# Transposing the activations of two of nine units by DMA in 16-bit halves instead of on TensorE

## The chip, the cores and the metric

The kernel runs on one core of one Trainium2 chip. The metric is the time of one execution on the device, in microseconds (us). Before the change it is 636.36 us, the median of 3 runs (635.49 to 636.7).

## What is computed

The reference is an attention followed by a dense layer pair and a soft mixture of experts:

```python
attn_out = _attn_ref(q, k, v, tau)            # 4 batches, 8 heads, 576 tokens, head size 64
x = attn_out.transpose(0, 2, 1, 3).reshape(2304, 512)
g = np.maximum(x @ w_in, 0.0) ** 2            # 2304 x 2048
x = g @ w_out                                 # 2304 x 512
logits = x @ phi                              # 32 slots
d = softmax(logits over the 2304 tokens)
slot_input = d.T @ x                          # 32 x 512, four slots for each of 8 experts
slot_out[e] = np.maximum(slot_input[e] @ w1[e], 0.0) @ w2[e]     # 512 -> 1024 -> 512
out = softmax(logits over the slots) @ slot_out                  # 2304 x 512
```

All inputs and outputs are 32-bit floats.

## The kernel before

**Units.** The 2304 tokens go through the dense layers in nine units of 256 tokens: two for each of the four batches, (0, 0) to (3, 1), and a last one, "rem", with the 64 tokens left over of each batch. So the seventh and eighth unit are the two of the last batch; the ninth is "rem". In each unit TensorE (PE) multiplies the split weights w_in with the unit's x (L1176, operations f_a and f_b, eight pairs; one pair gives 256 of the 2048 columns of g, transposed: columns of g on the partitions, the unit's 256 tokens along the free axis). ScalarE (ACT) applies relu (L1185) and square (L1193) into a tile `gt` of 128 x 512. There are nine gt buffers, and a unit has eight such tiles, so the next unit can begin only one pair before buffers of this one have to come free.

**The step after each unit.** `post` (L971) adds the rest of a unit's work, which is carried out while the next unit's f_a and f_b run. f_pl and f_pm (L982) multiply g with w_out @ phi for the logits; f_p12 and f_p1k (L989, L995) sum and turn them; f_alpha (L1005) takes the exponential; f_p3 (L273, L1041) turns the result, and DVE copies it to `dk` and `ar` (L1045, L1048). In place of x, the kernel accumulates d.T @ g (32 x 2048, in `sg`) and multiplies by w_out only at the end (L1344). For that g is needed with tokens on the partitions. f_turn transposes it on PE (L273, called from L1075): for each half t of the 256 tokens and each j of 0 to 3, four transposes of 128 x 128 into one PSUM tile, 32 transposes per unit. f_gk evacuates each of the eight PSUM tiles to a tile `gk` (L1083 on ACT, L1085 on VectorE (DVE) in part of the ninth unit); there are four gk buffers. f_acc (L1098) multiplies with dk, f_merge (L1107) adds into sg. The turns of t = 1 release the gt buffers.

**Order.** A planner at build time (class `Plan`) holds all operations of attention and of the units with their engine, a cost, dependencies, keys and buffers to acquire and release. It steps through time and starts on each free engine the ready operation with the lowest key; the order that comes out is the order of each engine's instructions, which the chip then executes with semaphores. For a DMA it keeps a `bus`, occupied for the given `dma` time; SP issues only while the bus is booked no further ahead than DQ = 2.212 us, and a DMA given with a negative time (a transpose) also holds SP's place:

```python
if o.dma:
    self.bus = max(self.bus, self.now + DMA_LEAD) + o.dma      # DMA_LEAD = 1.13
    o.end = max(self.bus, o.end + DMA_LEAD) + DMA_TAIL         # DMA_TAIL = 0.95
    if o.turn:
        self.free[o.eng] = max(self.now + o.cost, self.bus - DMA_TAIL)
```

**DMA transposes today.** In attention, the probabilities of the batches after the first, split into two 16-bit parts of 128 x 2304 (`hl`), are already transposed by DMA on SP's queue (dturn, L779), 48 times.

**Loads of the experts' part.** Eight tiles `raw64` (128 x 4 KB per partition) serve w_in, w_out, then q and k, and at last eight loads of 512 KB of w_out rows (w_pre, planned behind the stores of w_out; L1243). When attention is planned to its end, nine loads of 1 MB and one of 512 KB of expert rows (`ew8`, `ew6`) are issued at once into the memory that attention used; loads into buffers of x (`wx`) and of w_in (`w8`) are planned as these come free. The part after the units (`tail`) is written in program order: L1344 multiplies sg by the w_out rows, L1366 is the experts' first layer, L1421 the second, L1440 the output; further loads wait there for buffers that these steps release.

Of the kernel before, what the change touches and what calls it, by code (L numbers as in the profile page):

```python
# [147 lines left out]
def tile_kernel(  # L148
# [31 lines left out]
    RB = 8  # L180
# [21 lines left out]
    PORT = {('w_id', 'POOL'), ('low', 'POOL'), ('w_times', 'POOL'), ('w_rest', 'POOL'), ('spread', 'POOL'), ('c_low', 'POOL'), ('keep', 'DVE'), ('xhi', 'DVE'), ('xlo', 'DVE'), ('c_low', 'DVE'), ('c_shift', 'DVE'), ('w_lo', 'DVE'), ('v_lo', 'DVE'), ('q_lo', 'DVE')}  # L202
    FKEY = 1e5
    GKL = (1, 3)
    GKD = ()
# [84 lines left out]
    def row512(dt=F32, tag="gk", bufs=GB):  # L290
        return rows.tile([128, 512], dt, tag=tag, name=tag, bufs=bufs)

    def gt_tile():
        return fs.tile([128, 2 * NU], F32, tag="gt", name="gt", bufs=MC // 2 + 1)
# [10 lines left out]
    def conv_ops():  # L305
# [168 lines left out]
        for n in range(RB):  # L474
            add("w_pre", "SP", 0.5, lambda: state["wr"](), stores, 1000.0 + n, ["raw64"], dma=1.46)

# [484 lines left out]
    def ffn_ops(units):  # L961
# [8 lines left out]

        def post(u, d, first, last):  # L971
            w, po = {}, {}
# [92 lines left out]
            if not last:  # L1065
                codes(bk)
            lastsg, turns = fo.get("sg"), []
            for t in range(T):
                gks, ro = [], []
                for j in range(NG):  # L1070
                    def turn(t=t, j=j):
                        po[t, j] = mm_tile()
                        for i in range(MC // NG):
                            m = (MC // NG) * j + i
                            transpose(po[t, j][:, i * 128:(i + 1) * 128], d["gt"][m][:, t * 128:(t + 1) * 128])  # L1075

                    own = last and t == T - 1
                    tag = "cv" if own else "gk"

                    def evac(t=t, j=j, own=own, tag=tag):  # L1080
                        gk = w["gk", t, j] = row512(F32, "cv", CB) if own else row512()
                        if j not in gkd:
                            nc.scalar.activation(gk, po[t, j], AF.Copy)  # L1083
                        else:
                            nc.vector.tensor_copy(gk, po[t, j])  # L1085

                    rel = [("gt", d["rl"][2 * j + x]) for x in range(2)] if t == T - 1 else []
                    takes = ["mm", tag]
                    tt = add("f_turn", "PE", 0.47, turn, d["sq"], pk(), takes, rel)
                    gks.append((tag, tt))  # L1090
                    dv = j in gkd
                    ro.append(add("f_gk", "DVE" if dv else "ACT", 0.6 if dv else 0.49, evac, [tt], HI + 2, rel=[("mm", tt)]))
# [34 lines left out]
        for n, u in enumerate(units):  # L1127
# [33 lines left out]
            for m2 in range(MC // 2):  # L1161
# [21 lines left out]
                def relu(m2=m2, d=d, o=o, down=down):  # L1183
                    g = o["g"] = gt_tile()
                    nc.scalar.activation(g, o["h"], AF.Relu, scale=down)  # L1185
                    d["gt"][2 * m2], d["gt"][2 * m2 + 1] = g[:, 0:NU], g[:, NU:2 * NU]
# [20 lines left out]
            plan.release(ms[-1], [("xh", hs[0]), ("xl", ls[0])])  # L1207
            pending = lambda u=u, d=d, n=n: post(u, d, n == 0, n == len(units) - 1)
        pending()
# [252 lines left out]
    with tc.manual_schedule():  # L1462
        with ExitStack() as ph:
# [9 lines left out]
            W, take, ew8, ew6, wr, wx, w8, wg = weights()  # L1473
            state["wr"] = wr
            conv_ops()
            attn_ops()
# [5 lines left out]
        state["ew"] = ctx.enter_context(tc.tile_pool(name="ew", bufs=9, side="right"))  # L1482
        for f in [ew8] * 9 + [ew6]:
            f()
        for n in range(XPB + 1):
# [40 lines left out]
```

## Time and profile before

| | before |
|---|---|
| median of 3 runs | 636.36 us (635.49 to 636.7) |
| profiled execution, its own time | 636.38 us |
| its span in the trace | 634.6 us |
| PE busy | 580.7 us (92%) |
| DVE, ACT, POOL busy | 435.1, 438.9, 283.7 us |
| attention's last step | ends at 480.6 us |
| f_pl of seventh, eighth, ninth unit | at 495.7, 526.7, 557.7 us |
| L1344, first step with w_out rows | at 570.1 us |
| last load of expert rows lands | at 615.0 us |

Times in the trace are counted from the start of the span; the rows sit in engines' lanes named PE, PEld (weight loads of PE), DVE, ACT, POOL and SP (which issues the DMAs; SPq is its queue). A name such as `gk<-mm` is the tile written and the tile read. "Share" of the DMA is the mean over the core's 16 DMA engines.

### The profile page before, as it was taken

What the parts mean: (1) busy time and instruction counts of PE and PEld (TensorE: products, weight loads), DVE (VectorE), ACT (ScalarE), POOL (GpSimd) and SP (SyncE); (2) the same over time, 40 slices, a digit from 0 to 9 for tenths busy, and PEclk for the clock granted to TensorE, in tenths of its full rate; (3) what the DMA queues carried; (4) which work ended last, traced back from release to release, by engine and by line L of the source; (5) the groups of instructions that cost most, each with busy time, mean ns of one, the idle gap of its engine ahead of it and who ended that gap; (6) DMA issues with size and microseconds to landing.
All of it is one profiled execution on the core that took longest, in us unless ns stands there. A gap on an engine that the chain in (4) does not pass through costs nothing.

```text
span 634.6 us, 14115 instructions
## 1 busy us (share of the span) xinstructions
PE 580.7 (92%) x5218; PEld 405.8 (64%) x5218; DVE 435.1 (69%) x1230; ACT 438.9 (69%) x846; POOL 283.7 (45%) x464
## 2 busy tenths in 40 slices
PE   3897979989999999999999989999999999989972
PEld 1454546667777677667767667867868787854322
DVE  5798998999988987886888977897640302042133
ACT  3797757688888888988988878887864545431012
POOL 1446672267577766676756767765530000010000
PEclk9999888999999999999999999999999999999987
DMA  8975516667787867595856747787656911568957
GB/s 279 354 224 170 189 67 207 212 180 174 210 145 160 184 134 140 97 195 100 185 106 118 175 91 151 125 181 165 144 76 254 400 77 34 173 223 325 419 222 297
DMA packets 150324, 116.78 MB, mean 184 GB/s; under 512 B 119920, under 2 KB 128880, under 8 KB 148080
## 3 DMA queue, kind: packets, MB, share of 16 engines
q1 hardware_dynamic: 150256, 115.88, 67.3%
q8 instruction: 41, 0.67, 0.4%
q14 instruction: 27, 0.22, 0.1%
HBM read 73.72 MB, written 8.91 MB: 130 GB/s over the span
## 4 chain that ended last, share of the span: by engine, by line
PE 61%; DVE 15%; DMA 7%; ACT 6%; POOL 5%; issue 3%; SPq 1%; DVEq 0%; ACTq 0%; POOLq 0%
PE mm L1176 27%; PE mm L273 8%; PE s L707 6%; DMA w<-in_moe_w_dram 5%; PE po L876 5%; DVE u L733 4%; DVE e L749 4%; PE mm L1098 2%; POOL hl L772 2%; PE po L868 2%; PE mm L982 2%; ACT e L745 2%; PE s L694 2%; PE po L881 1%; DMA qt<-in_q_dram 1%
## 5 line engine op out<-in xcount | busy, mean ns | idle before, releaser
L1176 PEld LDWEIGHTS <-w 128*128 128x128 f16 x1728 | 166.5, 98 | 26.8 <-issue 7.9
L772 POOL TENSOR_TENSOR hl<-e,hl 128x288 f16<-128x288 f32 x192 | 147.2, 791 | 39.0 <-issue 28.5
L1176 PE MATMUL mm<-xh,w 128*128 128x256 f16 x1152 | 149.6, 273 | 0.3 <-ACT gk L1083 0.2
L749 DVE SCALAR_TENSOR_TENSOR e<-u,sm,e 128x576 f32<-128x576 f32 x144 | 120.1, 850 | 18.9 <-ACT e L745 14.7
L745 ACT ACTIVATE e<-u,sm 128x576 f32<-128x576 f32 x144 | 109.1, 770 | 20.3 <-DVE u L733 15.1
L739 POOL TENSOR_SCALAR sm<-sm,tau_p 128x1 f32<-128x1 f32 x144 | 72.9, 512 | 70.4 <-DVE u L733 64.3
L1176 PE MATMUL mm<-xl,w 128*128 128x256 f16 x576 | 86.4, 273 | 0.0
L1185 ACT ACTIVATE gt<-mm,scl 128x512 f32<-128x512 f32 x72 | 49.2, 683 | 53.4 <-PE mm L1176 52.8
L733 DVE TENSOR_SCALAR_CACHE_REDUCE u<-s,raw 128x576 f32<-128x576 f32 x90 | 71.1, 811 | 14.2 <-PE s L707 13.2
L768 ACT ACTIVATE hl<-e 128x576 f16<-128x576 f32 x96 | 64.0, 676 | 1.7 <-DVE e L749 1.5
L836 POOL TENSOR_SCALAR sm<-sm 128x4 f32<-128x4 f32 (+1 forms) x48 | 20.4, 426 | 61.1 <-DVE e L749 51.5
L1193 ACT ACTIVATE gt<-gt 128x512 f32<-128x512 f32 x72 | 45.0, 625 | 1.1
L733 DVE TENSOR_SCALAR_CACHE_REDUCE u<-s,nscale 128x576 f32<-128x576 f32 x54 | 42.6, 807 | 3.7 <-PE s L694 3.2
L1318 POOL MEMSET cv<- 128x512 f32 x4 | 1.9, 526 | 96.5 <-PE mm L1098 96.5
L816 ACT ACTIVATE pt<-mm 128x512 f32<-128x512 f32 x48 | 28.5, 601 | 19.8 <-PE mm L273 19.3
L1083 ACT ACTIVATE gk<-mm 128x512 f32<-128x512 f32 x66 | 35.3, 593 | 7.2 <-PE mm L273 7.0
L707 PEld LDWEIGHTS <-qt 128*128 128x128 f16 (+3 forms) x400 | 21.9, 99 | 28.5 <-issue 18.0
L273 PE MATMUL mm<-ident_r,e 128*128 128x128 f32 (+1 forms) x224 | 37.4, 301 | 2.8 <-DVE e L749 2.2
L273 PE MATMUL mm<-ident_r,gt 128*128 128x128 f32 x288 | 38.0, 278 | 0.2 <-ACT gk L1083 0.2
L273 PEld LDWEIGHTS mm<-ident_r,e 128*128 128x128 f32 (+1 forms) x224 | 28.1, 154 | 15.6 <-DVE e L749 5.4
L273 PEld LDWEIGHTS mm<-ident_r,gt 128*128 128x128 f32 x288 | 31.7, 143 | 8.0 <-issue 6.0
L876 PE MATMUL po<-pt,vh 128*64 128x256 f16 x576 | 36.0, 275 | 0.0
(196 smaller groups left out, 974.5 us busy)
## 6 DMA issues: line engine op xcount, KB each, us to landing
w<-in_moe_w_dram SPq DMA_DIRECT2D x17, 1024.0 KB, 14.0
w<-in_moe_w_dram SPq DMA_DIRECT2D x26, 512.0 KB, 8.7
raw<-in_moe_w_in_dram SPq DMA_DIRECT2D x16, 511.8 KB, 6.7
raw<-in_moe_w_out_dram SPq DMA_DIRECT2D x16, 511.8 KB, 4.1
raw<-in_v_dram SPq DMA_DIRECT2D x20, 256.0 KB, 3.4
w_out<-cv SPq DMA_DIRECT2D x16, 256.0 KB, 2.6
w<-w_out SPq DMA_DIRECT2D x8, 512.0 KB, 4.2
kt<-in_k_dram SPq DMA_DIRECT2D x10, 320.0 KB, 3.6
```

The lines of the kernel that those rows point to most:

```text
L273: nc.tensor.transpose(out_, in_, ident[:n, :n])
L707: nc.tensor.matmul(o0, d["qh"][r, a, q0], kk, start=full, stop=not full)
L733: nc.vector.tensor_scalar(u, o["s"][:, s0:s0 + S], d.get("nscale", nscale), None, ALU.mult, ALU.min, accum_out=gd["sm"][:, c:c + 1])
L739: nc.gpsimd.tensor_scalar(sm[:, 4 + c:5 + c], sm[:, c:c + 1], tau_p, None, ALU.add)
L745: nc.scalar.activation(e, o["u", a], AF.Exp, scale=-1.0, bias=gd["sm"][:, c:c + 1])
L749: nc.vector.scalar_tensor_tensor(e, o["u", a], sm[:, 4 + c:5 + c], e, ALU.is_le, ALU.mult, accum_out=sm[:, 8 + c:9 + c])
L768: nc.scalar.activation(o["hl"][:, a * S:(a + 1) * S], o["e"][:, a * S:(a + 1) * S], AF.Copy)
L772: nc.gpsimd.tensor_tensor(o["hl"][:, 2 * S:][:, i], o["e"][:, i], o["hl"][:, i], ALU.subtract)
L876: nc.tensor.matmul(po[64 * a:64 * a + 64, :n_], d["vh"][:, y, c0:c0 + D], gd["pt"][:, :, c + 5 * a + m, :], start=i == 0 and m == 0, stop= ...
L1176: nc.tensor.matmul(o["h"][:, i * NU:(i + 1) * NU], a, c, start=n_ == 0, stop=n_ == len(terms) - 1)
L1185: nc.scalar.activation(g, o["h"], AF.Relu, scale=down)
L1193: nc.scalar.activation(g, g, AF.Square)
```

## The change

For the seventh and eighth unit (`DTU = (6, 7)`, counted from 0) g is not transposed on PE. For each j, two f_part on ACT copy the two gt tiles of a pair, taken as 16-bit words, into one raw64 tile, upper and lower halves of each word apart; f_move transposes that tile of 128 x 2048 words by one DMA on SP into a second raw64 tile; f_join on DVE puts the halves together again into gk, in two copies for each t and j. gt buffers are released by f_part and f_pm. The w_out loads get a later key and stand behind these in the line for raw64 (which rows they load is fixed ahead, in `wo`), and the ew loads are planned as operations, with a place on the bus, instead of being issued at once.

```diff
+    DTU = (6, 7)
+    DEA = (0, 1)
...
+    def row512x2():
+        return rows.tile([128, 4 * CW], U16, tag="raw64", name="raw64", bufs=RB)
...
-            add("w_pre", "SP", 0.5, lambda: state["wr"](), stores, 1000.0 + n, ["raw64"], dma=1.46)
+            add("w_pre", "SP", 0.5, lambda n=n: state["wr"](state["wo"][n]), stores, 2 * FKEY + n, ["raw64"], dma=1.46)
...
+            halves = {}
+            for j in range(NG) if by_halves else ():
+                o = {}
+
+                def part(x, j=j, o=o):
+                    t = row512x2()
+                    if not x:
+                        o["h"] = t.rearrange("p (h x n) -> p h x n", h=2, x=2)
+                    else:
+                        o["t"] = t.rearrange("p (b f) -> p b f", f=128)
+                    g = d["pair"][2 * j + x].bitcast(U16).rearrange("p (n h) -> p h n", h=2)
+                    if x in DEA:
+                        nc.scalar.activation(o["h"][:, :, x], g, AF.Copy)
+                    else:
+                        nc.vector.tensor_copy(o["h"][:, :, x], g)
+
+                def move(j=j, o=o):
+                    nc.sync.dma_start_transpose(out=o["t"], in_=o["h"].rearrange("p h x n -> p (h x n)"))
+
+                hs = []
+                for x in range(2):
+                    eng = "ACT" if x in DEA else "DVE"
+                    hs.append(add("f_part", eng, 1.05 if x in DEA else 1.13, lambda x=x, f=part: f(x), [d["sq"][2 * j + x]] + hs[:1],
+                                  pk(), ["raw64"]))
+                    plan.release(hs[x], [("gt", d["rl"][2 * j + x])])
+                    plan.release(a, [("gt", d["rl"][2 * j + x])])
+                halves[j] = o, add("f_move", "SP", 1.0, move, hs, HI, [], [("raw64", hs[0])], dma=-3.5), hs[1]
             for t in range(T):
                 gks, ro = [], []
                 for j in range(NG):
...
+                    if by_halves:
+                        def join(t=t, j=j):
+                            gk = w["gk", t, j] = row512()
+                            y = gk.bitcast(U16).rearrange("p (m f h) -> p h m f", m=4, h=2)
+                            z = halves[j][0]["t"].rearrange("p (h m t) f -> p t h m f", h=2, t=T)[:, t]
+                            for h in range(2):
+                                nc.vector.tensor_copy(y[:, h], z[:, h])
+
+                        rel = [("raw64", halves[j][2])] if t == T - 1 else []
+                        r = add("f_join", "DVE", 1.2, join, [halves[j][1]], pk(), ["gk"], rel)
+                        gks.append(("gk", r))
+                        ro.append(r)
+                        continue
...
-            pending = lambda u=u, d=d, n=n: post(u, d, n == 0, n == len(units) - 1)
+            pending = lambda u=u, d=d, n=n: post(u, d, n == 0, n == len(units) - 1, n in DTU)
...
+            state["wo"] = [take(1024) for _ in range(RB)]
...
-        for f in [ew8] * 9 + [ew6]:
-            f()
+        for n, f in enumerate([ew8] * 9 + [ew6]):
+            add("w_load", "SP", 0.5, f, [], n - 100, dma=2.6 if f is ew8 else 1.3)
```

## Rows read from the trace of the kernel before

**Rows 1.** The page: busy time of PE, and its row of 40 slices.

```profile
PE 580.7 (92%) x5218; PEld 405.8 (64%) x5218; DVE 435.1 (69%) x1230; ACT 438.9 (69%) x846; POOL 283.7 (45%) x464
...
PE   3897979989999999999999989999999999989972
```

**Rows 2.** Stretches from f_pl to f_pl, and the tail: length, engines busy, PEclk, DMA share, GB/s.

```profile
495.70:526.68 30.98, 30.57 (x284) 24.49 (x283) 6.30 (x21) 15.92 (x29) 0.00 (x0) 1.00 0.49 191
526.68:557.65 30.97, 30.56 (x284) 24.48 (x283) 5.24 (x17) 15.91 (x29) 0.00 (x0) 1.00 0.36 120
...
583.00:615.00 32.00, 28.12 (x218) 9.16 (x210) 8.34 (x27) 2.96 (x6) 0.00 (x0) 0.95 0.91 371
```

**Rows 3.** The chain that ended last: start, length, what (seventh unit's post; the tail).

```profile
497.84 1.02 PE mm L273 x8
...
499.97 0.91 PE mm L273 x8
500.88 2.62 PE mm L1176 x24
...
505.41 1.90 PE mm L273 x16
...
570.12 3.57 PE mm L1344 x32
...
583.26 0.22 SPq L1243
...
583.57 16.09 DMA w<-in_moe_w_dram
```

**Rows 4.** The page's group of g's transposes; PE's timeline at the seventh unit's first f_acc.

```profile
L273 PE MATMUL mm<-ident_r,gt 128*128 128x128 f32 x288 | 38.0, 278 | 0.2 <-ACT gk L1083 0.2
...
504.34 1.06 PE L1098 MATMUL mm<-gk,dk 128*32 128x512 f32 x8 [0.41 <-DVE ar L1048]
```

**Rows 5.** Groups by form, ACT and DVE: busy us, mean ns, idle before.

```profile
L1083 ACT ACTIVATE gk<-mm 128x512 f32<-128x512 f32 x66 | 35.3, 593 | 7.2 <-PE mm L273 7.0
L335 ACT ACTIVATE raw<-raw 128x512 f16<-128x512 bf16 x16 | 21.6, 1364 | 10.6 <-DMA raw<-in_moe_w_in_dram 10.1 <-DMA raw<-in_moe_w_out_dram 0.4
L914 ACT ACTIVATE rr<-mm 128x256 f32<-128x256 f32 x32 | 12.0, 375 | 0.9 <-PE mm L273 0.7
...
L333 DVE CAST raw<-raw 128x512 f16<-128x512 bf16 x16 | 14.4, 951 | 0.0
L339 DVE TENSOR_SCALAR raw<-raw 128x512 int32<-128x512 uint32 x32 | 13.0, 429 | 1.5 <-DMA raw<-in_moe_w_in_dram 1.5
```

**Rows 6.** Line 779, the DMA transposes of attention: us from issue to landing.

```profile
DMA to landing us min/median/max: 4.6/4.7/6.3
```

**Rows 7.** DMA issues by tile (KB each, median us to landing), then SP's timeline.

```profile
w<-in_moe_w_dram SPq DMA_DIRECT2D x17, 1024.0 KB, 14.0
w<-in_moe_w_dram SPq DMA_DIRECT2D x26, 512.0 KB, 8.7
...
w<-w_out SPq DMA_DIRECT2D x8, 512.0 KB, 4.2
...
443.18 6.01 SPq L1243 DMA_DIRECT2D w<-w_out  x2
```

**Rows 8.** Stretches for the DMA engines, the last two columns: DMA share, GB/s.

```profile
480.64:615.00 134.36, 127.40 (x1125) 83.57 (x1123) 29.52 (x93) 48.11 (x88) 1.92 (x4) 0.99 0.66 251
480.64:508.00 27.36, 26.95 (x253) 22.16 (x252) 5.93 (x21) 14.50 (x27) 0.00 (x0) 1.00 0.97 383
508.00:540.49 32.49, 32.08 (x298) 25.84 (x297) 5.24 (x17) 16.02 (x30) 0.00 (x0) 1.00 0.14 51
462.44:468.00 5.56, 5.56 (x56) 4.21 (x54) 2.71 (x13) 3.90 (x10) 0.26 (x1) 1.00 0.57 106
...
470.57:476.57 6.00, 6.00 (x55) 4.58 (x54) 2.18 (x7) 3.38 (x6) 0.00 (x0) 1.00 0.82 101
449.36:457.50 8.14, 8.14 (x87) 7.29 (x88) 5.17 (x23) 7.62 (x17) 3.43 (x7) 1.00 0.99 210
```

More of the change, by code (lines that the diff above doesn't have):

```diff
@@ L969, in ffn_ops, with post @@
         HI = -1e5
-        def post(u, d, first, last):
+        def post(u, d, first, last, by_halves):
             w, po = {}, {}
@@ L1184, in relu @@
                     g = o["g"] = gt_tile()
+                    d.setdefault("pair", {})[m2] = g
                     nc.scalar.activation(g, o["h"], AF.Relu, scale=down)
```

## The prediction

> **What bounds the kernel now.** I read the page's engine line and its 40 slices first: TensorE (PE) is busy 92% of the span, and from the seventh slice to the thirty-eighth its slices stand at 9, but for three at 8 [rows 1]. Then the stretches of the last three units, cut where the seventh, eighth and ninth unit's activations go into f_pl: PE is busy 30.57 of 30.98 us and 30.56 of 30.97 us, its granted clock is 1.00 throughout (the 2.4 GHz level), while ACT is busy 15.9 and DVE 5 to 6 us [rows 2]. Then the chain, which in these stretches is PE instructions nearly end to end [rows 3]; the one wait of PE is 0.41 us for dk and ar, two small DVE copies, once per unit [rows 4]. So from the end of attention (480) to the end of the ninth unit whatever leaves PE leaves the time, unless something new makes PE wait. From 583.57 on the chain is loads of expert rows, the first piece of it 16.09 us long, the next like it [rows 3]; the DMA engines are busy 0.91 of that stretch [rows 2]. That tail starts from PE: SP's piece just ahead, at 583.26, is the issue of loads whose buffers L1366 releases [rows 3], so it moves with PE as long as the DMA engines have finished all earlier loads by then.
>
> **What leaves PE.** For units seven and eight the f_turn transposes go. One unit has 32; in the chain they are pieces of 8, 8 and 16 that advance it by 1.02, 0.91 and 1.90 us, together 3.83 us [rows 3], 120 ns each. Two units: **7.66 us**. The page gives 278 ns as the mean of one [rows 4], but neighbours overlap, and the chain counts what they cost. "TensorE: Matmul & The Clock Gate", Part 4, of the Trainium skill gives some 275 ns for a transpose in one kernel's context; the trace's 278 ns agrees as a duration, but taken as a price it would make the estimate 17.6 us for 64, and the chain does not bear that out.
>
> The dk wait goes for free: f_acc must now wait for f_join anyway and is planned behind further f_a and f_b, by when dk is long there. That is 0.41 us a unit [rows 4], 0.82 at most; I take half, 0.4, since other short waits (l4 before f_p12, dT before f_p3) lose the transposes that filled them. Their filler is f_a and f_b of the next unit, which only need a free gt buffer, and these come free early: f_part of a pair runs as soon as its square is done, so six of eight before f_pl; f_pm does the rest.
>
> **What is added.** Per unit:
> - ACT: 8 f_part, 1024 elements each, in place of 8 f_gk at 0.593 us [rows 5]. Bounds for one: from 256 to 512 elements an ACT copy grows from 0.375 to 0.593 us, so 1024 would take 1.03 us; 512 elements with a step of 8 bytes took 1.364 us [rows 5], so 1024 could take 2.6 (twice that, less the 0.16 that the first two rows leave at no elements). f_part reads with a step of 4 bytes and writes without a step, nearest to the first: 1.03 us, as the plan's 1.05. ACT then does 15.9 - 4.7 + 8.2 = 19.4 us in 31: covered. If the high end held, it would be 32 in 31 and no cover left.
> - DVE: 8 f_join of two copies of 512 16-bit elements, written with a step of 4 bytes. For one copy: 0.429 us (32-bit, step 8 bytes, both operands in SBUF) to 0.951 us (16-bit, step 8 bytes) [rows 5]; I take the plan's 0.60 between them, 1.2 per join and 9.6 us a unit, in a DVE that works 6 us in 31 [rows 2].
> - DMA: 4 f_move, 2048 columns. The transposes of attention have 2304 and land 4.6 to 6.3 us after issue, median 4.7 [rows 6]; scaled by 16/18 some 4.2 us. The plan reckons 1.13 + 3.5 + 0.95 = 5.6 us and reserves the queue for it, so that the order in which PE's instructions are written leaves 1.4 us of reserve. PE is not stopped by any of this: each f_acc stands in PE's order where the plan expects its joins, and f_a and f_b of the next unit (2.62 us for one of its eight pairs [rows 3], 21 us per unit) stand ahead of it. The last move of a unit starts some 2 us after its last square, lands 4 to 6 us later, one join, f_acc; then four joins of t = 1 (gk has four buffers, so these wait for the first f_acc) and the second f_acc: about 15 us after f_pl, half a unit.
>
> **What is moved.** SP's queue. Ten ew loads, so far issued in one go after attention, and the eight 512 KB loads of w_out rows, so far issued by 449 [rows 7], now stand behind the moves; the w_out loads need the raw64 buffers of the eighth unit, which come free with its joins, at about 533. On SP a move waits for its f_part, and what is queued behind it are these loads; POOL's queue has nothing in these stretches [rows 2]. The first that PE needs of them is w_out's, in L1344 (570 now, 562 then). Does it fit? From 480.64 to 615 the engines are busy 0.66 of 134.4 us, 45.7 us are free, most of it between 508 and 540 (share 0.14) [rows 8]. With the end 8.1 us earlier 37.6 remain. To be put in: the w_out rows, 8 x 0.524 MB at 395 GB/s (383 GB/s at a share of 0.97 [rows 8]), 10.6 us; and eight moves. One lone transpose occupied 0.57 of 5.56 us, 3.2 us; another, of 470.6, came to 0.82 of 6 us, 4.9 us [rows 8]. Scaled: 2.8 or 4.4 us, 22 or 35 us for eight. I take the lower, since the pair from 449.36 with half a megabyte beside it also came to at most 3.4 each (0.99 of 8.14 us less 1.3) [rows 8]. That makes 33 of 37.6 us: it fits, without much room. In order of time: ew, the first three xp loads and the moves fill the engines from 481 to about 533, then the remaining xp load, eight w8 and eight w_out loads (17 x 1.3 us) take until about 555, 7 us before L1344.
>
> **Sum.** 7.66 + 0.4 = 8.06 us off the profiled execution's 636.38 us (its span is 634.6; it lies 0.02 us from the median of the runs, 636.36): **628.3 us**.
>
> **The rivals.**
> 1. *The copies are slower than planned and PE waits for f_acc.* With 0.951 us a copy a join takes 1.9, not 1.2. The first f_acc is covered by the move's 1.4 us, the second comes four joins later: 4 x 0.7 = 2.8 us per unit, 5.6 for both: 633.9 us. For: the 16-bit copies with a step are the slow ones on both engines [rows 5]. Against: those steps were 8 bytes.
> 2. *The DMA engines are full.* At 4.4 us a move 35 + 10.6 = 45.6 us are to go into 37.6: 8 us too many, w_out's rows reach L1344 late by that, and the gain is gone: 636.3 us. For: the transpose of 470.6. Against: the two other readings.
> 3. *Slower: the moves land among queued loads.* Half-megabyte loads that were queued behind others landed after 8.7 us, megabyte loads after 14.0 [rows 7]. If the last move of unit seven lands after 14.0 and that of unit eight after 8.7, PE stands 8.4 + 3.1 = 11.5 us before f_acc: +3.4, 639.8 us. It decides from 8.1 us of such waits in all. For: SP will have megabyte loads in flight at every move of unit seven. Against: the plan lets SP issue only while its backlog is 2.2 us or less, and the transposes of attention ran beside loads too and never took over 6.3 us [rows 6]. "VectorE: DVE Perf Modes" of the Trainium skill, Rules for kernel authors, says the contrary of this change: transpose on TensorE where PSUM is an acceptable destination, by DMA otherwise; the section on the three transpose paths gives 1309 ns for a 128x128 bf16 block by DMA, by which an estimated 16 blocks are 21 us a move and this rival would hold by far. The trace disagrees: 18 blocks land in 4.7 us, 0.26 us a block.
> 4. *It does not do what it says*, if f_join or f_part left the order of the units as it is with the transposes still there: the diff's `continue` skips them, so this has next to no chance.
>
> **How the numbers follow.** Forecast 0.66, rival 1 0.14, rival 2 0.11, rival 3 0.08, rival 4 0.01. A measurement of this kernel can tell about 0.2% (1.3 us) from no change. The forecast and rival 1 are faster; rival 2 I split 0.04 faster, 0.05 same, 0.02 slower around its 636.3; rival 3 is slower, rival 4 the same. So faster 0.84, same 0.06, slower 0.10. Range: downwards the whole dk wait (627.9) and half the spread of the runs (0.6): 627.3; upwards rival 1's 633.9. Rivals 2 to 4, 0.20 together, stay outside.
>
> **What would show it.** Right: no f_turn transposes between f_pl of the seventh and of the ninth unit, these stretches at 26.7 to 27.2 us each (31.0 less 3.83, and up to 0.41) with PE busy throughout and the clock at 1.00; f_part near 1.03, f_join's copies 0.4 to 0.6 us, moves landing in 4 to 5.6 us; a free stretch on the DMA queues before L1344; the same DMA pieces at the end, 8 us earlier. Wrong: PE idle before L1098 released by f_join (rival 1) or by a move (rival 3); PE idle before L1344 released by a w_out load, or longer waits of L1421 for expert rows (rival 2).

## The result, and the profile after

Over 16 runs each the changed kernel took 630.50 us (median; 627.66 to 635.46) and the kernel before 635.68 us (634.45 to 640.6): a ratio of 0.9915, with an interval of 0.9895 to 0.9935. Ratios and their intervals are taken over executions in the chip's faster state alone, and need not be the quotient of the medians. That is 5.4 us less by the ratio (4.1 to 6.7), where 8.06 were forecast. The direction and the mechanism held, the time lies inside the range, and about two thirds of the sum arrived. The profiled execution of the changed kernel took 629.16 us (span 627.0, 2.16 us around it; before 636.38, 634.6 and 1.78).

First the page of the changed kernel, its engine line and the DMA row of the 40 slices, which answer to [rows 1]:

```profile
PE 574.6 (92%) x5154; PEld 397.8 (63%) x5154; DVE 448.3 (71%) x1262; ACT 446.9 (71%) x846; POOL 286.6 (46%) x464
...
DMA  8965526666888667686866755565545998999968
```

PE has 64 instructions less, the transposes of two units, and is 6.1 us less busy; its share of the span is still 92%. DVE has 32 more (16 joins of two copies). Next the stretches, with the columns of [rows 2] (length, busy PE, PEld, DVE, ACT, POOL, PEclk, DMA share, GB/s): the seventh and the eighth unit's, the time of all loads, a part of attention, the w_out step and its first part, and the last loads:

```profile
496.48:523.47 26.99, 26.99 (x254) 20.79 (x258) 11.31 (x35) 19.04 (x29) 0.00 (x0) 1.00 1.07 277
523.47:550.46 26.99, 26.99 (x254) 20.77 (x258) 10.05 (x31) 12.76 (x22) 0.00 (x0) 1.00 0.94 301
...
481.00:607.00 126.00, 120.94 (x1064) 76.25 (x1062) 40.62 (x124) 55.52 (x89) 1.92 (x4) 0.99 1.00 328
400.00:450.00 50.00, 49.35 (x509) 36.94 (x509) 38.42 (x104) 41.75 (x81) 33.11 (x53) 1.00 0.53 98
...
562.79:568.06 5.27, 5.27 (x34) 1.22 (x34) 1.50 (x5) 0.00 (x0) 0.00 (x0) 0.68 0.93 337
...
562.79:566.10 3.31, 3.31 (x17) 0.80 (x20) 1.50 (x5) 0.00 (x0) 0.00 (x0) 0.50 1.05 391
...
577.90:607.45 29.55, 26.58 (x214) 8.46 (x205) 8.10 (x27) 2.17 (x4) 0.00 (x0) 1.00 0.95 391
```

The two units take 26.99 us each instead of 30.98 and 30.97 [rows 2], PE busy without a gap and at clock 1.00 in both. ACT does 19.0 us in the first of them, DVE 11.3. So the part that the prediction was about went as it said: 7.97 us less. The DMA engines, which stood at 0.14 between 508 and 540 before [rows 8], are now at 1.00 on average from 481 to 607. And two rows show something that was not forecast: PE is idle for 0.65 us between 400 and 450, inside attention, and the w_out step has a mean clock of 0.68, 0.50 in its first 3.31 us.

The chain that ended last (start, length, what), as in [rows 3]:

```profile
506.75 4.04 PE mm L1221 x36
510.78 0.99 PE mm L1143 x8
511.78 7.97 PE mm L1221 x72
519.74 0.99 PE mm L1143 x8
...
562.86 5.20 PE mm L1390 x32
...
570.47 7.17 PE mm L1412 x64
577.63 0.22 SPq L1289
...
577.94 15.66 DMA w<-in_moe_w_dram
...
593.62 13.82 DMA w<-in_moe_w_dram
```

In the seventh unit's stretch both f_acc (now L1143) stand among f_a and f_b (L1221) with nothing ahead of them that waits, and no transposes of g (L275). In the tail the w_out step (L1390) takes 5.20 us, where the same step took 3.57 [rows 3]. The rest keeps its form: L1412 releases buffers, SP issues loads, and two pieces of loads end the kernel. They start at 577.94 instead of 583.57 [rows 3], 5.63 us earlier, and last 29.5 us instead of 31.4 (583.57 to the last landing at 615.0). So in these two executions 1.9 us of the difference come from loads that ran a little slower in the profile of before, which is no merit of the change; more on this below.

The lines of the new operations, f_part, f_move and f_join (min/median/max in ns, first and last start):

```profile
L1085 ACT ACTIVATE raw<-gt x16: 1040/1057/1057, 473.7 to 524.9; 128x1024 uint16<-128x1024 uint16 x16
...
L1090 SPq DMA_TRANSPOSE raw<-raw x8: 1932/3532/5550, 483.3 to 526.0; - x8
...
DMA to landing us min/median/max: 4.3/5.4/8.3
...
L1125 DVE COPY gk<-raw x32: 439/449/459, 491.7 to 539.3; 128x512 uint16<-128x512 uint16 x32
...
its engine sat idle before it (us, times) until:
  DMA raw<-raw: 14.6, 4
```

f_part 1.06 us, f_join's copies 0.45 us, the moves 4.3 to 8.3 us to landing. DVE stood 14.6 us waiting for moves, and it cost nothing, since DVE has that to spare and the chain does not pass through it.

SP's timeline (start, length, operation, count) shows how loads and moves share its queue:

```profile
477.62 1.30 SPq L1289 DMA_DIRECT2D w<-in_moe_w_dram  x3
483.26 8.31 SPq L1090 DMA_TRANSPOSE raw<-raw  x2
...
504.57 2.44 SPq L1289 DMA_DIRECT2D w<-in_moe_w_dram  x4
513.14 15.48 SPq L1090 DMA_TRANSPOSE raw<-raw  x4
528.67 10.60 SPq L1289 DMA_DIRECT2D w<-in_moe_w_dram  x9
...
550.92 2.69 SPq L1289 DMA_DIRECT2D w<-w_out  x5
```

The megabyte loads go out a few at a time between the moves. The last w_out load is issued at 553.2, and the view of the DMA issues around that time has its time to landing in the last column:

```profile
w<-w_out SPq DMA_DIRECT2D x1, 512.0 KB, 10.1
```

So it lands at 563.3, half a microsecond after L1390 has begun. L1390 takes its rows in a fixed order and reads this load first with the 23rd of its 32 matmuls, at 566.2 in the trace: 2.9 us later.

### The profile page after: what moved, and what is told of

Read it like the earlier page. It is cut to its first block, busy times and chain, and to the rows that moved or that the text cites. A ratio compares the mean times of both kernels' runs of the same rounds, so it can differ in the third digit from the quotient of the medians.

```text
span 627.0 us, 14027 instructions
## 1 busy us (share of the span) xinstructions
PE 574.6 (92%) x5154; PEld 397.8 (63%) x5154; DVE 448.3 (71%) x1262; ACT 446.9 (71%) x846; POOL 286.6 (46%) x464
## 5 line engine op out<-in xcount | busy, mean ns | idle before, releaser
L1221 PEld LDWEIGHTS <-w 128*128 128x128 f16 x1728 | 166.7, 99 | 29.5 <-issue 10.2
L777 POOL TENSOR_TENSOR hl<-e,hl 128x288 f16<-128x288 f32 x192 | 149.1, 800 | 38.0 <-issue 26.8
L1221 PE MATMUL mm<-xh,w 128*128 128x256 f16 x1152 | 150.5, 274 | 0.2 <-ACT gk L1115 0.2
L754 DVE SCALAR_TENSOR_TENSOR e<-u,sm,e 128x576 f32<-128x576 f32 x144 | 121.6, 860 | 17.2 <-ACT e L750 13.7
L1221 PE MATMUL mm<-xl,w 128*128 128x256 f16 x576 | 86.9, 274 | 0.0
L275 PE MATMUL mm<-ident_r,e 128*128 128x128 f32 (+1 forms) x224 | 36.4, 295 | 2.7 <-DVE e L754 2.2
L275 PEld LDWEIGHTS mm<-ident_r,e 128*128 128x128 f32 (+1 forms) x224 | 27.2, 151 | 15.8 <-DVE e L754 5.3
L712 PE MATMUL s<-kt,qt 128*128 128x512 f16 (+1 forms) x200 | 32.9, 289 | 2.4 <-DVE u L738 2.2
L881 PEld LDWEIGHTS <-vh 128*64 128x64 f16 x576 | 29.6, 110 | 5.1 <-issue 4.4
L712 PE MATMUL s<-raw,qt 128*128 128x64 f16 (+1 forms) x200 | 31.2, 294 | 0.0
```

Of the source, the lines that this page charges most:

```text
L275: nc.tensor.transpose(out_, in_, ident[:n, :n])
L712: nc.tensor.matmul(o0, d["qh"][r, a, q0], kk, start=full, stop=not full)
L754: nc.vector.scalar_tensor_tensor(e, o["u", a], sm[:, 4 + c:5 + c], e, ALU.is_le, ALU.mult, accum_out=sm[:, 8 + c:9 + c])
L777: nc.gpsimd.tensor_tensor(o["hl"][:, 2 * S:][:, i], o["e"][:, i], o["hl"][:, i], ALU.subtract)
L881: nc.tensor.matmul(po[64 * a:64 * a + 64, :n_], d["vh"][:, y, c0:c0 + D], gd["pt"][:, :, c + 5 * a + m, :], start=i == 0 and m == 0, stop= ...
L1221: nc.tensor.matmul(o["h"][:, i * NU:(i + 1) * NU], a, c, start=n_ == 0, stop=n_ == len(terms) - 1)
```

## The experiments

Executions of one and the same program differ by several us, and most of that arises early: the first unit's f_pl lies between 201.9 and 210.0 us in the traces below, though the instructions up to there are the same. So traces are compared from the first f_pl on. This table is worked out from PE's timeline of each profiled execution (us; "tail" is from the ninth f_pl to the end of the span; a w_out step of 3.57 us belongs to a clock of 1.00; "around the span" is the execution's own time less its span, which is given to 0.1 us):

| kernel | 1st to 7th f_pl | 7th to 8th | 8th to 9th | w_out step | tail | around the span |
|---|---|---|---|---|---|---|
| before | 292.82 | 30.98 | 30.97 | 3.57 | 76.95 | 1.78 |
| before, again | 292.82 | 30.98 | 30.97 | 3.57 | 74.7 | 1.82 |
| before, filled | 292.79 | 30.97 | 30.98 | 3.57 | 75.2 | 1.77 |
| after | 293.54 | 26.99 | 26.99 | 5.20 | 76.6 | 2.16 |
| after, again | 293.58 | 26.99 | 26.99 | 5.27 | 76.6 | 2.18 |
| order only | 292.78 | 30.97 | 30.97 | 5.17 | 76.8 | 1.83 |
| seventh unit only | 293.56 | 26.98 | 30.98 | 3.57 | 75.1 | 1.76 |
| ew loads at once | 293.58 | 44.01 | 26.98 | 5.01 | 76.4 | 2.11 |
| place kept | 292.84 | 28.42 | 26.99 | late loads | 77.8 | 2.14 |
| place kept, filled | 292.81 | 28.21 | 26.99 | late loads | 78.6 | 2.10 |
| after, filled | 293.58 | 26.99 | 26.98 | 3.57 | 75.1 | 2.15 |
| half loads, filled | 293.58 | 26.98 | 26.99 | 3.57 | 75.5 | 2.10 |
| sixth and seventh | 297.49 | 26.99 | 30.97 | 3.57 | 74.7 | 1.88 |

**The change again**, unaltered, so that the next three kernels stand beside it on the same chip.

> The changed kernel unchanged, for its spread and a second trace. Two theories of why the median gain is 5.2 to 5.5 us where the two units' stretches gave 7.97 in the trace. P: the rest is lost in the tail to TensorE's granted clock, which fell to 0.50 in L1390 in the trace (1.6 us) and more often elsewhere; then executions of 628 and of 634 us differ by their mean clock, and the DMA stretch at the end is as long in both. D: the DMA engines are full from 530 to the last load, so that the end is set by bytes; then the median of 630.5 comes back, and the last load lands at about 607 to 610 whatever the clock does.

629.94 us (7 runs) against 636.65 (24 runs), ratio 0.9904 [0.9869, 0.9938]: the first measurement holds. The trace repeats that of after in every column, the slow w_out step and the 293.58 us ahead of the seventh f_pl included, so neither is an accident of one execution.

**Order only**: no unit is turned by DMA; the planned ew loads and the later key of the w_out loads stay.

```diff
-    DTU = (6, 7)
+    DTU = ()
```

> No unit by DMA; the w_out loads' late place and the planned ew loads stay. All 32 transposes per unit are back on TensorE. P: 0 against the kernel before, +-1 us, 635 to 636.5 us: the loads only move into idle DMA time. D: the w_out loads add 10.6 us of transfers behind the eighth unit, so that part of the tail's loads come later: 1 to 3 us slower than before, 637 to 639 us.

636.51 us (12 runs), ratio 0.9997 [0.9965, 1.003]. So without the moves the new planning of loads alone gives and costs nothing that could be measured. The run tests less than it was meant to: SP's timeline has the w_out loads from 365.3 to 456.3, inside attention as before (with no moves ahead of them in the line for raw64 they found free buffers at once). Only the planned ew loads were tested. What it shows besides: 292.78 us ahead of the seventh f_pl, as before, while the w_out step is slow with all transposes in place, so that step's price does not hang on the transposes.

**Seventh unit only.**

```diff
-    DTU = (6, 7)
+    DTU = (6,)
```

> Only the seventh unit by DMA, the eighth on TensorE as before: four moves instead of eight, 64 - 32 transposes gone. P: half of the units' gain, 4.0 us against the kernel before, 631.7 us by the medians, and 2 to 4 us less gain than the full change in the units' stretches. D: the DMA engines have 12 us less to do, so the tail starts with no loads in arrears and all 4.0 us arrive, while the full change gets little for its second unit: 631 to 632 us here, within 1.5 us of the full change.

633.02 us (12 runs), ratio 0.9957 [0.9938, 0.9976]: 2.7 us less (1.5 to 3.9), half of what two units give. The trace has 26.98 us in the seventh's stretch, 30.98 in the eighth's: 4.0 us per unit, and each unit by itself. The 0.74 us ahead of the seventh f_pl are there in full with one unit (293.56), so this term is not per unit.

**The ew loads at once**, as in the kernel before; everything else as in the change.

```diff
-        for n, f in enumerate([ew8] * 9 + [ew6]):
-            add("w_load", "SP", 0.5, f, [], n - 100, dma=2.6 if f is ew8 else 1.3)
+        for f in [ew8] * 9 + [ew6]:
+            f()
```

> The two units by DMA, but the ten ew loads issued at once after attention, as before the change. If moves queue behind the loads that SP issued ahead of them, the seventh unit's moves land up to 24 us late (10 MB at 0.4 MB per us); PE's order has at most some 8 us of f_a ahead of the first f_acc beyond the move's own time, so PE waits 10 to 18 us before it: 640 to 648 us, a slower kernel than before. If transfers on the queue share the engines, the moves take perhaps twice their time and PE waits 2 to 5 us: 633 to 636 us.

647.17 us (5 runs), ratio 1.0173 [1.0144, 1.0203]: 11 us slower than before, 17 slower than the change. All of it lies in one stretch, the seventh unit's, 44.01 us instead of 26.99. The chain of this kernel there:

```profile
499.84 8.76 SPq L1090
...
508.70 4.58 DMA raw<-raw
...
513.37 0.79 DVE gk L1125 x2
514.16 0.37 DVE xl L1192
```

And the landings of its moves, from the view of their line (L1090):

```profile
DMA to landing us min/median/max: 4.2/5.3/16.0
```

SP sends twelve loads from 478.23 on and then the first moves. The first of these holds SP for 14.0 us, until 508.6, and lands 16.0 us after its issue; the second can only be issued behind it, at 508.7, and lands at 513.3. f_join (L1125) waits for these moves at the head of DVE's queue, and behind f_join in that queue stands xl, the low half of the next unit's x (L1192), which has no need of the move: PE waits 14.4 us in one go for xl. In the whole stretch PE is busy 29.23 us instead of 26.99, at a mean granted clock of 0.84 instead of 1.00, which is most of the rest of the 17 us. So the third rival's mechanism exists, with another victim than it named: not f_acc, which has a reserve, but what is queued behind the waiting copy on DVE. The paced ew loads are what keeps it away in the change.

**Place kept.** From here three theories for the missing 2 to 3 us stand against each other. O: the w_out loads leave attention's plan, and without them the planner writes the last part of attention in another order, worse by 0.7 us. C: the w_out step runs at a lower granted clock. D: the DMA engines, at a share of 1.00, set the end. For O, eight operations that issue nothing stand in the plan where the w_out loads were, with their key, cost and place on the bus:

```diff
+            place = add("w_place", "SP", 0.5, lambda: None, stores, 1000.0 + n, ["raw64"], dma=1.46)
+            plan.release(place, [("raw64", place)])
+        for n in range(RB):
             add("w_pre", "SP", 0.5, lambda n=n: state["wr"](state["wo"][n]), stores, 2 * FKEY + n, ["raw64"], dma=1.46)
```

> The full change, with eight operations in the plan that do nothing, at the key, cost and bus time that the w_out loads had in attention: the order of attention's instructions is then the one of the kernel before up to the seventh unit's post. Theory O (the new order of attention's last part makes PE wait): the seventh unit's f_pl comes 292.8 us after the first one's as before, not 293.5, and the kernel gains 0.7 us against the changed one, some 6.3 us against the kernel before. Rival (the 0.7 us come from the transfers or copies themselves): 293.5 us again and no gain. Both leave the two units' stretches at 27.0 us.

632.23 us (12 runs) against 636.94 (29 runs), ratio 0.9926 [0.9902, 0.995], no better than the change. But the traces split it. Two rows of PE's timeline of the changed kernel have the only waits that this view names between 400 and 500:

```profile
413.80 1.50 PE L987 MATMUL mm<-gt,wphi 128*32 128x256 f32 x24 [0.52 <-ACT gt L1231]
467.58 0.69 PE L873 MATMUL po<-pt,raw 128*64 128x64 f32 x16 [0.21 <-ACT pt L821]
```

The windows of the kernel with the place kept:

```profile
400.00:450.00 50.00, 50.00 (x523) 36.93 (x521) 38.72 (x109) 41.43 (x81) 32.76 (x55) 1.00 0.56 100
450.00:494.93 44.93, 44.93 (x446) 36.43 (x444) 16.53 (x56) 33.55 (x59) 9.05 (x15) 1.00 0.63 123
494.93:523.35 28.42, 27.16 (x251) 20.64 (x250) 11.14 (x36) 19.04 (x29) 0.00 (x0) 1.00 1.08 294
```

With the place kept PE waits for nothing up to the seventh f_pl, which comes 292.84 us after the first, as before: O is shown, 0.74 us. The waits of the change are short ones of PE for ACT (0.52 in the fifth unit's f_pl, 0.21 for a copy of attention), 0.73 us together, made by the new order of instructions and not by a moved transfer. (What the place keeps is the key, the cost, the bus and the buffer of these loads together; which of them sets the order was not tried.) This order costs more elsewhere, though. In the seventh's stretch PE now waits 1.3 us for dT (28.42 instead of 26.99), and the w_out loads come late, as the chain from 552.71 on shows:

```profile
552.71 8.91 DMA w<-w_out
561.69 7.36 DMA w<-in_moe_w_dram
569.12 8.93 DMA w<-in_moe_w_dram
578.11 16.54 DMA w<-in_moe_w_dram
```

And PE's timeline has a wait for a w_out load inside the w_out step, at the matmul that reads the last load first:

```profile
565.72 1.90 PE L1393 MATMUL mm<-w,gk 128*32 128x512 f32 x10 [0.20 <-DMA w<-w_out]
```

The step runs from 562.74 to 567.62 at a granted clock of 1.00, 1.2 us longer than where no load is late. Here loads follow loads to the end: D holds in this kernel, whose last w_out load lands at 565.7 instead of 563.3, and the tail is 77.8 us.

**Place kept, filled**: the same, with the filling that is explained next.

> As e5_place, and in the tail five matmuls on a constant tile ahead of the one that waits 1.2 us for rs (their result is used by nobody). Theory C (the granted clock falls to 0.50 in L1390's lines because PE stood still 0.4 and 1.2 us just before): the clock stays at 1.00 there, the step takes 3.6 instead of 5.2 us, and 1 to 1.6 us are gained: 7.5 us against the kernel before. Rival (the end is set by the bytes to load, D): the step gets shorter and the loads at the end last longer by as much: no gain over e5_place.

631.51 us (12 runs), ratio 0.9933 [0.9906, 0.996], the tail 78.6 us. The filling gives nothing here, and it could not: in the kernel with the place kept the clock had not fallen in the w_out step, which waits for late loads. So this run does not bear on C.

**Before, one more trace**, unaltered, to see whether the tail of the first is typical.

> The kernel before, unchanged, for a second trace of it. Theory O: from its first f_pl to its seventh 292.8 us as in the first trace. Theory C: L1344 takes 3.6 us or, where the granted clock falls, 5.2; the stretch from the ninth f_pl to the last load is 55.4 us where the clock stays up throughout and about 57 where it falls once.

635.92 us (one execution); the tail is 74.7 us instead of 76.95. So the profile shown of before has a tail that is 2.2 us longer than this one, in the loads and not in the w_out step. From the ninth f_pl to the last landing it is 57.4 us in the first trace and 55.1 in this one, with the clock at 1.00 in the w_out step of both: a stretch of 57 us is no sign of a fallen clock by itself, as the expectation took it to be. A difference of two traces therefore flatters the change: 7.22 us between the two profiled executions.

**After, filled.** For C: ahead of the w_out step PE stands 1.2 us for rs, a DVE result, and then 0.39 us in the matmul with it. Five matmuls of 128 x 128 that nobody reads are put into this gap, ahead of the one that waits for rs:

```diff
+        for _ in range(5):
+            nc.tensor.matmul(p0[:, 128:256], stack_f, stack_f, start=True, stop=True)
```

> The changed kernel with the five matmuls in the tail alone (no places in the plan of attention, so the order up to the tail is the changed kernel's). Theory C (what the tail loses is the granted clock in L1390): the clock stays at 1.00 there, L1390 takes 3.6 instead of 5.2 us, and from the ninth f_pl to the last load's landing it is 55.4 us, as in the kernel before where its clock stays up, instead of 57.0; 1.6 us gained, 6.8 to 7 us against the kernel before. Theory D (the DMA engines are full from 481 on and the bytes set the end): 56.5 to 57 us again and nothing gained.

629.55 us (12 runs) against 636.22 (23 runs), ratio 0.9906 [0.9879, 0.9932]. The w_out step, L1392 in this kernel, in its windows:

```profile
562.99:566.56 3.57, 3.57 (x33) 0.94 (x34) 1.50 (x5) 0.00 (x0) 0.00 (x0) 1.00 1.05 389
```

The end of its chain:

```profile
576.12 0.22 SPq L1289
...
576.43 15.69 DMA w<-in_moe_w_dram
...
592.14 13.82 DMA w<-in_moe_w_dram
```

The clock stays at 1.00, the step takes 3.57 us again, the issue of the last loads comes at 576.12 instead of 577.63 (with a ninth f_pl that is 0.13 us later), and the two pieces of loads behind it are as long as in the change, 15.69 and 13.82 us. The tail is 75.1 us instead of 76.6. So what the fallen clock costs is shown in the traces: 1.5 to 1.6 us, passed on in full to the end. That it is the filling which holds the clock rests on two traces of the changed kernel without it, where the clock fell, and two with it (this one and the one with half the loads), where it did not; over all kernels without filling it fell in four traces of nine, so chance is not excluded. The medians (629.55, and 629.94 and 630.50 for the change) do not separate the two kernels; how often the clock falls in executions without a profile is open.

**Before, filled**: the same five matmuls in the kernel before, whose clock did not fall in either trace.

> The kernel before with the five matmuls in the tail. Theory C: where the clock does not fall in L1344 in this kernel, as in its first trace, nothing is gained, 0 +-0.8 us; if it falls in most of its executions, 1 to 1.6 us.

635.86 us (12 runs), ratio 0.9992 [0.9968, 1.0017]; w_out step 3.57 us, tail 75.2. Where the clock stands, filling gives nothing, so what the filled trace of the changed kernel gains is not from some other effect of five more matmuls.

**Half loads, filled.** For D in the change: the nine loads of 1 MB bring only half of their rows, and the other half of the experts' weights in them is taken to be the same (this kernel thus computes with other weights).

```diff
-            nc.sync.dma_start(out=t, in_=part(kind, e, k0, n))
+            few = 1 if tag == "ew8" and len(state["half"]) < 9 else n
+            state["half"] += [tag] * (tag == "ew8")
+            nc.sync.dma_start(out=t[:, 0:few], in_=part(kind, e, k0, few))
...
-                W[r] = t[:, i, :]
+                W[r] = t[:, min(i, few - 1), :]
```

> As e6_filled, but each of the nine 1 MB loads after attention brings only half of its rows, the others being taken as the same: 4.7 MB, some 11 to 12 us of transfers, are left out of the stretch from 481 on, at the same places in the queues. D: the engines are no longer full, the loads before the tail are done in time, and from the ninth f_pl to the last landing it is 55.4 us or less: 1.6 us or more faster than e6_filled. C: the same as e6_filled within 0.5 us.

629.72 us (6 runs), ratio 0.9906 [0.9878, 0.9934], as the filled kernel with all loads. The windows of this kernel over the time of these loads (the same stretches of the filled one have shares of 1.11 and 1.00):

```profile
480.00:508.00 28.00, 28.00 (x265) 22.90 (x265) 8.00 (x24) 20.04 (x29) 0.00 (x0) 1.00 0.79 180
508.00:540.00 32.00, 32.00 (x296) 24.18 (x294) 12.88 (x41) 20.73 (x32) 0.00 (x0) 1.00 0.72 190
```

The engines become a quarter free, and the tail stays (75.5 against 75.1 us). The last w_out load is issued 2.8 us after the ninth f_pl, as in the change, so it is not the full engines that hold its issue back. So D falls for the change as far as the loads before the tail go: a share of 1.00 there is work that PE does not wait for. The last two pieces of loads, behind L1412, end the kernel as before.

**Sixth and seventh unit** instead of seventh and eighth, that is, one unit further into attention:

```diff
-    DTU = (6, 7)
+    DTU = (5, 6)
```

> The sixth and seventh unit by DMA instead of the seventh and eighth: the sixth's four moves then run in attention's last part, where the engines are busy only 0.3 to 0.8, and the w_out loads get their buffers one unit (27 us) earlier. D: 12 us of transfers less after 481, so the tail is as long as in the kernel before (55.4 us to the last landing), and if attention bears f_part and f_join beside its own work (ACT and DVE are busy 0.7 to 0.9 there) the gain is 7 us, 1.5 us more than the change's. C: no better than the change; worse by what PE waits in attention for the slower ACT and DVE, 0 to 3 us.

637.86 us (12 runs), ratio 1.001 [0.9984, 1.0036]: no gain, from the same operations. The seventh unit gives its 4.0 us (26.99). But the first to the seventh f_pl take 297.49 us, though the sixth unit's 32 transposes are gone from there: 3.95 us more than in the change, where some 4 less were due. PE's timeline in this kernel shows where:

```profile
463.62 0.63 PE L987 MATMUL mm<-gt,wphi 128*32 128x256 f32 x4 [1.55 <-ACT gt L1239]
464.98 0.62 PE L994 MATMUL mm<-l,stack_f 128*32 128x256 f32 x2 [0.73 <-ACT l L1057]
467.89 0.42 PE L275 MATMUL mm<-ident_r,dT 32*128 32x32 f32 x2 [1.73 <-ACT dT L1010]
```

The window around these waits:

```profile
425.00:475.00 50.00, 45.40 (x439) 33.14 (x442) 35.18 (x107) 40.01 (x73) 26.96 (x42) 0.93 0.70 123
```

All three waits end with ACT, which is 80% busy there with attention's exponentials. The first two are instructions that stood behind others on ACT: a square behind copies of attention and an f_part, and the copy of the logits (L1057) right behind an f_part, as ACT's timeline has it:

```profile
463.60 1.06 ACT L1085 ACTIVATE raw<-gt 128x1024 uint16<-128x1024 uint16 x1
464.56 0.36 ACT L1057 ACTIVATE l<-mm 128x256 f32<-128x256 f32 x1
```

The third is not ACT's load: ahead of dT, ACT itself stood still for 2.35 us, released by DVE. In that window of 50 us PE is busy 45.4 us, and its granted clock has a mean of 0.93. In the kernel before the same window has PE busy throughout at 1.00:

```profile
425.00:475.00 50.00, 50.00 (x508) 37.15 (x506) 32.33 (x100) 37.21 (x75) 24.51 (x43) 1.00 0.65 130
```

The 4.6 us of idle time and, as an estimate, 0.07 of 45.4 us for the clock, 3.2 us, make up nearly all of the 8 us. That ACT's load is the cause is read from this trace; no run tried it by itself, and the planner's order changed here too.

## Why the prediction was right, and where its size was off

**What leaves PE** was right. 7.66 us of transposes and 0.4 for the waits for dk were reckoned, 8.06 in all; the two stretches are 7.97 us shorter, 26.99 us each, inside the 26.7 to 27.2 that were named. 120 ns for a transpose, taken from the chain and not from the 278 ns of the group, was the right price: 32 of them and half of the 0.41 us of [rows 4] make 4.04 per unit, and 3.98 came.

**What is added** was hidden, as said. f_part took 1.06 us where 1.03 was taken from the row without a step, and the bound of 2.6 was far off. f_join's copy took 0.45 where 0.60 was taken between 0.43 and 0.95, so the first rival had no ground. The moves landed in 5.4 us in the median; 4.2 had been scaled from [rows 6], and the plan's 5.6 was nearer. The longest took 8.3. It was covered: the last join ahead of the seventh unit's first f_acc ends at 508.1, 2.6 us before that f_acc, and the second f_acc stands 23.3 us after f_pl, where the prediction reckoned about 15. The trace again disagrees with the price of a block in "VectorE: DVE Perf Modes", The three transpose paths, of the Trainium skill, 1309 ns: 16 blocks in 5.4 us are 0.34 us a block, a quarter of it. The rule under "Rules for kernel authors" there, TensorE where PSUM is an acceptable destination, is turned round in the seventh and eighth unit, where PE is the bound and 4.0 us per unit were gained. In the sixth, where nothing was gained, it held.

**What is moved** was half right. The loads were in time, and L1390 did not wait. But the reckoning that 33 of 37.6 us of free engine time would be used, with the w_out rows in place by 555 and 7 us to spare, was too rosy: the share is 1.00 from 481 to 607, 0.97 from 530 to 563, where a free stretch ahead of L1390 was to be a sign of being right, and the last w_out load lands at 563.3, 2.9 us ahead of its first reader. The mis-sized term is the engine time of a move. By the shares 126.0 us are now busy instead of 88.7 (0.66 of 134.4); less 10.6 for the w_out rows, 26.7 us are left for eight moves, 3.3 each (an estimate) where 2.8 were taken and 4.4 was the rival's. The w_out loads also go out later, from 539.3 to 553.2, where the prediction let their buffers come free at about 533. The second rival's premise, full engines, is thus true; its price is not, since half of nine large loads could go without any gain. How near it lies is shown by the kernel with the place kept, where loads in a slightly other order set the end.

**The third rival** did not come, for the reason given against it, the pacing of SP by the plan: with the ew loads issued at once it comes, and costs 17 us, more than the 11.5 reckoned, since it stops the next unit's f_a and f_b and not only f_acc.

**The sum** came out 2.7 us above what was gained, by terms that it did not hold. It took 8.06 us from one stretch and let everything else stand or "move with PE". Three things did not:

- The w_out loads leave attention's plan, and the prediction costed that only as DMA time. The planner also reorders all that is left: +0.72 us ahead of the seventh f_pl, shown by putting their place back.
- "Moves with PE" held for the last loads, but PE itself lost 1.6 us in the w_out step by its clock. The prediction had the clock at 1.00 in the units and did not ask for it behind them. The trace with the gap filled has the 1.6 us back. Against the two traces of before without filling, whose tails are 76.95 and 74.7 us, 75.8 in the mean, the change's 76.6 is only +0.8, since the last loads of the first of them ran slow. That the clock fell is not the transposes' doing: it fell with all of them in place too (order only).
- The time around the span grew, as all executions on record show, from 1.79 us in the mean (before) to 2.13 (the change), +0.34. The means are 2.11 to 2.18 in every kernel with the seventh and the eighth unit turned by DMA and 1.78 to 1.85 in all others. What makes it was not tried.

Together -7.97 + 0.72 + 0.8 + 0.34 = -6.1 us, beside -5.4 (4.1 to 6.7 less) and, in the second measurement, -6.1 (3.9 to 8.3 less). That the sum comes near is in part luck: the first profile of before, with its long tail, gives 7.22, the second one 5.0: the mean tail of before is the least certain term.

## What to carry to other kernels

Work that is taken off the bound engine pays where the engines that get it have spare time and where nothing short is queued behind their waits: the same three operations gave 4.0 us per unit behind attention, took the gain back when one of the two units stood inside attention, and cost 17 us when a waiting copy stood ahead of the next unit's operand. Price a pipelined instruction by what the chain advances (120 ns), not by its own duration (278 ns), and pace loads that share a queue with transfers that someone waits for. When the order of instructions comes from a planner, an operation that is moved away changes the order of all that remains, and the terms of a sum have to include the stretches that were not touched, their waits and their granted clock.

## What the runs showed of the hardware beyond that

**The granted clock in the w_out step.** PE's clock fell to 0.50 (1.2 GHz) at the beginning of the w_out step in after, after again, order only and ew loads at once, and stayed at 1.00 (2.4 GHz) in both traces of before, in seventh only, in sixth and seventh, and with the place kept. In the changed kernel's windows it stood there for 3.31 us, in which PE did 17 of the step's matmuls. Ahead of it PE had stood still for 1.2 us, and the matmul with rs takes 0.39 us of the chain; this is the same in the unfilled kernels that kept the clock. With the gap filled, it stayed in all four traces, two of them of kernels that keep it anyway. In the kernel with the sixth unit by DMA it fell elsewhere: to a mean of 0.73 between 463 and 470, where PE was busy 3.92 of 7 us. What decides between the unfilled kernels is open.

**A transpose holds its queue.** One DMA transpose occupied SP's queue for 1.9 to 5.6 us in the change, and for up to 14.0 us behind twelve queued loads. **DMA shares over 1**: the seventh's stretch reads 1.07 at 277 GB/s, the tail 0.95 at 391 GB/s, so with transposes under way the share says little about the bytes that still fit. **16-bit copies with a step**: writing with a step of 4 bytes took DVE 0.45 us for 512 elements, against 0.95 for the 16-bit row in [rows 5]. That row reads and writes with a step of 8 bytes and also converts the type, so the runs do not tell which of these makes the difference.
